# Key sums of three of sixteen blocks by transfers into the other head's sum tile

## The chip, the cores and the metric

The kernel runs on one core of a Trainium2 chip. Its time is the device time of one execution in microseconds; the median of the runs of the kernel before is 2820.77 us (three runs, 2820.2 to 2821.47).

## What is computed

Two blocks are applied to the same input `x` (2048 rows of 1024) and mixed by a gate for each row: A is a linear-attention block, B a softmax-attention block, both with 32 heads of 32 columns.

```python
def _A_ref(x, wqkv, wo):
    qkv = (x @ wqkv).reshape(B, S, 3, H, Dh).transpose(2, 0, 3, 1, 4)
    q, k, v = qkv[0], qkv[1], qkv[2]
    phi = lambda t: jnp.where(t > 0, t + 1, jnp.exp(t)) + 1e-6
    pq, pk = phi(q), phi(k)
    kv = jnp.einsum("bhsd,bhse->bhde", pk, v)
    z = jnp.einsum("bhsd->bhd", pk)
    num = jnp.einsum("bhqd,bhde->bhqe", pq, kv)
    den = jnp.einsum("bhqd,bhd->bhq", pq, z)[..., None] + 1e-6
    return (num / den).transpose(0, 2, 1, 3).reshape(B, S, D) @ wo

def _B_ref(x, wqkv, wo):
    ...
    scores = jnp.einsum("bhqd,bhkd->bhqk", q, k) * (Dh ** -0.5)
    p = _softmax(scores, axis=-1)
    return jnp.einsum("bhqk,bhkd->bhqd", p, v).transpose(0, 2, 1, 3).reshape(B, S, D) @ wo

x = A_x
g = _sigmoid((x * gate_w).sum(-1, keepdims=True))
return g * _A_ref(...) + (1 - g) * _B_ref(...)
```

## The kernel before

PE does all products in fp32 or in three-term products of split operands. After a first part (the projections of B, up to about 620 us) the rest is one long interleaving of four streams, written out in advance by a planner in the kernel's own code: each engine has a booked clock in `T`, `use(engine, cost, ...)` moves it on, and in each turn the main loop takes the stream whose next step can begin soonest by those clocks. So a number such as the cost in `use("pool", 1.23, end)` runs nothing, but decides the order in which instructions stand on every engine.

The streams are:

- **lin** (`linear()`, matmuls L154, L157, L159): the projections of block A, in chunks, first keys and values (kind "kv", beside heads 0 to 14), then queries ("q", heads 14 to 19), then the output of A ("o", heads 19 to 30). At a change of chunk new weights are loaded by SP, split by a ScalarE cast (L1052) and a GpSimd subtraction (L1054) into two parts. For kv chunks the features of the keys are summed over all rows in `zsum` by GpSimd (L1329, L1331).
- **max** (`maxima()`): for each head, 64 score matmuls (L1440), each followed by DVE's row maximum of the bank (L1445). They run one head ahead.
- **head** (`heads_()`): for each head, 16 blocks of 128 keys by four quarters of 512 queries: score matmul (L1581), ScalarE's exp (L1584) into one of nine tiles `pr` of 128x2048, `slot(h, t) = (16 h + t) mod 9`. Blocks 0 to 7 and 8 to 15 are multiplied with the values in two groups (`av`, L1731).
- **out**: the output product of B at the end.

The softmax needs, for each query, the sum of the exps over the keys. It is built from the `pr` tiles in `lacc`, one of two tiles that alternate between heads (`lacc_t[h % 2]`). In heads with `qp = 1536` (all but 15 to 19 and 31), DVE adds the last 512 queries in a PSUM bank (`own`, L1682), and GpSimd the first 1536: block 0 and 1 in `first` (L1662), blocks 2 to 11 in `more` (L1666, 128x1536 each) and blocks 12 to 15 by quarters (`part`, also L1666, 128x512 each), as their exps come by quarters. When all are in, two accumulate DMAs issued by GpSimd fold the tile's halves onto each other (`fold`, L1620 and L1621), and PE sums over the partitions by a product with ones (`finish`, L1504; unfolded, L1496, for heads without fold, among them 30). For head 31 DVE adds everything (L1686).

A `pr` tile may be written again, nine blocks later, once its sums are done and its values multiplied: `pr_left[slot]` holds the marks of the sums still owed, and the head stream waits for them before a block's first score. The sums are queued in `sums_left` and written into GpSimd's order by `add_now` when its clock permits, folds by `fold_now`.

The finish of head h−1 stands on PE ahead of the first `av` group of head h: `av` waits for what is in `ends` and calls it.

## Time and profile before

| | |
|---|---|
| median of the runs | 2820.77 us |
| the profiled execution | 2822.18 us, span 2820.4 us |
| granted clock of PE, mean | 0.998 |
| sum of GpSimd's 128x1536 adds (L1666) | 926.3 us in 264 |
| sum of its 128x512 adds | 487.0 us in 380 |

The profile is that of the profiled execution; engines are PE (matmul), PEld (weight load), DVE, ACT (ScalarE), POOL (GpSimd) and SP. In rows of waits the columns are engine, output and line, what is waited for, then the sum in us, the number of waits and the longest. Rows of windows give the stretch, its length, the busy time of each engine with its instructions, the granted clock of PE, the share of the DMA engines and GB/s. Rows of groups give busy time, mean in ns and the idle time before them. A timeline row begins with start and length in us.

### The profile page before, as it was taken

Reading aid. Unit: us, or ns where it says so; the run is one execution under the profiler, and the core shown is the slowest. Engines: PE = TensorE matmul, PEld = TensorE weight load, DVE = VectorE, ACT = ScalarE, POOL = GpSimd, SP = SyncE. Lnnn points to the kernel's source line nnn. Section 1 sums busy time; section 2 is a strip of 40 time slices with the busy share of each in tenths; the row PEclk is TensorE's granted clock in tenths of the full one; section 3 lists DMA queues with packets and bytes.
Section 4 is the critical chain, followed back from the end, with each engine's and each line's share of the span. In section 5 each row is a group of like instructions: output and inputs, shape, how many; then the busy total and the mean of one; then the engine's idle time right before and its main releaser. Section 6 shows DMA issues by size and latency. Waiting matters only on the chain.

```text
span 2820.4 us, 46781 instructions
## 1 busy us (share of the span) xinstructions
PE 2796.0 (99%) x15784; PEld 2010.3 (71%) x15784; DVE 2268.8 (80%) x3713; ACT 1662.6 (59%) x3170; POOL 2102.9 (75%) x1145
## 2 busy tenths in 40 slices
PE   9999999999999999999999999999999999999999
PEld 8888888886666666676676777667666666666587
DVE  6697759688877888788888778777888888887678
ACT  4343433347666666676776667667767667676522
POOL 0152026459999999999999789989999999999100
PEclk9999999999999999999999999999999999999999
DMA  8588749673433334333344456656544454334674
GB/s 269 166 275 281 225 143 283 218 234 90 123 84 84 92 99 111 93 98 89 88 117 129 152 158 193 183 170 195 136 108 131 107 162 107 92 106 126 233 232 155
DMA packets 391291, 432.77 MB, mean 153 GB/s; under 512 B 105550, under 2 KB 237902, under 8 KB 389260
## 3 DMA queue, kind: packets, MB, share of 16 engines
q1 hardware_dynamic: 367116, 389.27, 45.9%
q0 software_dynamic: 21632, 36.32, 6.1%
q10 hardware_dynamic: 2304, 4.20, 0.4%
q8 instruction: 126, 2.06, 0.3%
q14 instruction: 113, 0.93, 0.1%
HBM read 287.31 MB, written 127.93 MB: 147 GB/s over the span
## 4 chain that ended last, share of the span: by engine, by line
PE 90%; DVE 4%; POOL 3%; DMA 2%; ACT 1%; issue 1%; SPq 0%; DVEq 0%; POOLq 0%; ACTq 0%
PE bank L1731 15%; PE bank L1581 15%; PE bank L1440 15%; PE bank L154 12%; PE bank L157 12%; PE bank L159 12%; PE bank L644 5%; POOL big L1666 3%; DVE mx L1445 2%; DMA big<-ra 1%; PE bank L1504 1%; PE bank L1234 1%; DVE big L1903 1%; DMA big<-big 1%; ACT big L1584 1%
## 5 line engine op out<-in xcount | busy, mean ns | idle before, releaser
L1666 POOL TENSOR_TENSOR big<-big,big 128x512 f32<-128x512 f32 (+2 forms) x694 | 1643.7, 2372 | 61.0 <-ACT big L1584 15.0
L1445 DVE TENSOR_REDUCE mx<-bank 128x1 f32<-128x512 f32 x2048 | 1283.1, 682 | 280.6 <-PE bank L1440 278.3
L1584 ACT ACTIVATE big<-bank 128x512 f32<-128x512 f32 x2048 | 1151.7, 604 | 334.2 <-PE bank L1581 276.1
L1440 PE MATMUL bank<-big,big 128*128 128x512 f32 x1888 | 738.0, 393 | 2.9 <-ACT big L1584 2.2
L1581 PE MATMUL bank<-big,big 128*128 128x512 f32 x1888 | 736.4, 395 | 3.6 <-ACT big L1584 2.9
L154 PE MATMUL bank<-big,big 128*128 128x512 f32 x1408 | 552.8, 393 | 2.6 <-ACT big L304 1.4
L157 PE MATMUL bank<-big,big 128*128 128x512 f32 x1408 | 549.7, 390 | 0.0
L159 PE MATMUL bank<-big,big 128*128 128x512 f32 x1404 | 548.2, 390 | 1.1 <-DVE big L299 1.1
L1731 PE MATMUL bank<-big,mid 128*32 128x512 f32 x4096 | 457.6, 596 | 0.0
L1581 PEld LDWEIGHTS bank<-big,big 128*128 128x128 f32 x1888 | 353.3, 188 | 128.6 <-issue 43.6
L1440 PEld LDWEIGHTS bank<-big,big 128*128 128x128 f32 x1888 | 354.4, 188 | 84.1 <-ACT big L1584 7.7
L1731 PEld LDWEIGHTS bank<-big,mid 128*32 128x32 f32 x4096 | 133.8, 110 | 281.9 <-issue 279.9
L154 PEld LDWEIGHTS bank<-big,big 128*128 128x128 f32 x1408 | 264.8, 188 | 66.8 <-ACT big L1584 5.2
L159 PEld LDWEIGHTS bank<-big,big 128*128 128x128 f32 x1404 | 263.7, 188 | 57.3 <-DVE big L299 2.4
L157 PEld LDWEIGHTS bank<-big,big 128*128 128x128 f32 x1408 | 264.9, 188 | 55.2 <-DVE big L299 0.2
L1682 DVE TENSOR_TENSOR bank<-bank,big 128x512 f32<-128x512 f32 x364 | 252.2, 693 | 13.6 <-ACT big L1584 6.4
L304 ACT CAST big<-mid 128x512 fp32r<-128x512 f32 (+1 forms) x169 | 100.5, 619 | 138.1 <-DVE mid L1850 72.4
L299 DVE TENSOR_TENSOR big<-mid,big 128x512 fp32r<-128x512 f32 (+1 forms) x138 | 96.1, 712 | 78.6 <-ACT big L304 78.1
L644 PE MATMUL bank<-big,big 128*128 128x512 f32 x672 | 152.6, 389 | 0.0
L1662 POOL TENSOR_TENSOR big<-big,big 128x1536 f32<-128x1536 f32 (+1 forms) x31 | 132.9, 4288 | 24.0 <-ACT big L1584 24.0
L644 PEld LDWEIGHTS bank<-big,big 128*128 128x128 f32 x672 | 126.1, 188 | 26.2
L1739 ACT COPY mid<-bank 128x512 f32<-128x512 f32 x32 | 18.8, 588 | 207.9 <-PE bank L1731 180.5
(197 smaller groups left out, 2424.5 us busy)
## 6 DMA issues: line engine op xcount, KB each, us to landing
big<-xs SPq DMA_DIRECT2D x202, 256.0 KB
big<-qk SPq DMA_DIRECT2D x705, 64.0 KB
qk<-mid SPq DMA_DIRECT2D x128, 256.0 KB
xh<-xs SPq DMA_DIRECT2D x102, 256.0 KB
big<-oA SPq DMA_DIRECT2D x86, 256.0 KB
xs<-big SPq DMA_DIRECT2D x64, 256.0 KB
oA<-mid SPq DMA_DIRECT2D x64, 256.0 KB
big<-big POOLq DMA_DIRECT2D x50, 256.0 KB, 5.0
```

Of the source, the lines that this page charges most:

```text
L154: yield nc.tensor.matmul(ps, sh, mh_, start=(kt == 0), stop=False)
L157: yield nc.tensor.matmul(ps, sh, ml_, start=False, stop=(late and last))
L159: yield nc.tensor.matmul(ps, sl, mh_, start=False, stop=last)
L644: nc.tensor.matmul(bank[at + i], x_, w_, start=(kt == u == 0 and not onto), stop=(kt == KH - 1 and u == 2), skip_group_check=onto)
L1440: nc.tensor.matmul(bank[b], q[:, t % TPC * P:(t % TPC + 1) * P], k[:, j * C:(j + 1) * C], start=True, stop=True)
L1445: nc.vector.tensor_reduce(m[:, t, j:j + 1], bank[b], AX.X, ALU.max)
L1581: nc.tensor.matmul(bank[b], k[:, t * P:(t + 1) * P], q_cols(h, j), start=True, stop=True)
L1584: nc.scalar.activation(pr_t[i][:, j * C:(j + 1) * C], bank[b], AF.Exp, scale=SCALE)
L1662: nc.gpsimd.tensor_add(lacc[:, :qp], pr(0)[:, :qp], pr(1)[:, :qp])
L1666: nc.gpsimd.tensor_add(lacc[:, sl], lacc[:, sl], pr(t)[:, sl])
L1682: nc.vector.tensor_add(lacc[:, qp:] if t == NT - 1 else l_b[:, :n], l_b[:, :n], src)
L1731: nc.tensor.matmul(av_b[j * DH:(j + 1) * DH, :], v[:, t, :], pr(t)[:, j * C:(j + 1) * C], start=(t == 0), stop=(t == NT - 1))
```

## The change

In the 25 heads with `qp = 1536` and h < 30 the sums of blocks 8, 9 and 10 (`CHAIN`) are no longer added by GpSimd. Block 8's first 1536 columns are copied by a DMA that ScalarE issues into the other head's sum tile `x`, which is free at that time; blocks 9 and 10 are added to it by accumulate DMAs that GpSimd issues; then one GpSimd add (`total`) puts `x` into `lacc`. Each step is booked behind the landing of the one before (6 us for the copy, 8 us for an accumulate), and each block's `pr` tile is free when its own transfer has landed. The first sum of the next head, which writes `x`, is preceded by what is left of the chain.

Besides, GpSimd's booked costs change (split 1.23 to 1.35, fold 2.0 to 2.45, features 0.69 to 0.78, adds by 0.06, the first add by 0.81), the features' sums are written into GpSimd's order later (`features_now`, at their booked end plus 1.5 us, or when their buffer is due), and in the last head the finish of head 30 no longer stands ahead of the first `av` group but of the second (`early`).

```diff
--- before.py
+++ after.py
@@ -43,6 +43,7 @@
 PIECE_STEPS, PIECE_REST = (4.0, 3.0), 2
 GATE_STEP, GATE_FROM = 2.0, 18.0
 LATE = 1.0
+CHAIN = (8, 9, 10)
@@ -202,6 +203,16 @@
 
     folds = deque()
 
+    chained = deque()
+
+    def chain_now(upto=None):
+
+        while chained and (upto is not None or chained[0][0]() <= T["pe"]):
+            _, fn, mark = chained.popleft()
+            mark.end = fn()
+            if mark is upto:
+                return
+
     def add_later(h, fn):
         mark = Later(None, 0.0, 0.0, 0, None)
         sums_left.append((h, fn, mark))
@@ -222,7 +233,9 @@
     def need(items):
 
         for item in items:
-            if item.end is None and item.fn is None:
+            if item.end is None and any(mark is item for _, _, mark in chained):
+                chain_now(item)
+            elif item.end is None and item.fn is None:
                 add_now(item)
                 assert item.end is not None
             elif item.end is None:
@@ -1050,7 +1063,7 @@
         hi, lo = wpart(k, 0), wpart(k, 1)
         end = use("act", 0.52, at, T["pe"] + LATENCY["pe"])
         nc.scalar.copy(hi, raw)
-        w_ready[k] = use("dve", 0.6, end) if eng is nc.vector else use("pool", 1.23, end)
+        w_ready[k] = use("dve", 0.6, end) if eng is nc.vector else use("pool", 1.35, end)
         eng.tensor_sub(lo, raw, f32(hi))
         raw_free[id(raw)] = w_ready[k]
 
@@ -1207,6 +1220,12 @@
             give(bs[r], 0.0, [defer(low, at)])
 
     z_end = [0.0, 0.0]
+    z_todo = deque()
+
+    def features_now(upto=None):
+        while z_todo and (z_todo[0][0] <= upto if upto is not None else z_todo[0][1] <= T["pe"]):
+            z_todo.popleft()[2]()
+
 
     def keysum(c):
 
@@ -1314,6 +1333,7 @@
                     renew(k)
             extra = iter(())
             e, r = mid[3 + n % 3], mid[6]
+            features_now(n - 3)
             if kind == "kv":
                 va = mid[7][:, (n % 2) * HC:(n % 2 + 1) * HC]
                 yield from keys_alone(n - 2)
@@ -1321,14 +1341,19 @@
                 use("act", 0.28, T["pe"] + LATENCY["pe"])
                 end = phi(ps, e, HC)
 
-                def more(end, c=c, t=t, e=e, ps=ps):
+                def more(end, n=n, c=c, t=t, e=e, ps=ps):
                     pk = e[:, :HC]
                     nc.vector.scalar_tensor_tensor(pk, pk, 1.0, ps[:, :HC], op0=ALU.min, op1=ALU.add)
-                    z_end[c % 2] = use("pool", 0.69, end)
-                    if t == 0:
-                        nc.gpsimd.tensor_copy(zsum[c % 2], pk)
-                    else:
-                        nc.gpsimd.tensor_add(zsum[c % 2], zsum[c % 2], pk)
+                    z_end[c % 2] = None
+
+                    def features():
+                        z_end[c % 2] = use("pool", 0.78, end)
+                        if t == 0:
+                            nc.gpsimd.tensor_copy(zsum[c % 2], pk)
+                        else:
+                            nc.gpsimd.tensor_add(zsum[c % 2], zsum[c % 2], pk)
+
+                    z_todo.append((n, end + 1.5, features))
 
                 todo = [defer(more, end, 0.34)]
                 give(b, 0.0, todo)
@@ -1619,7 +1644,7 @@
             need(lefts)
             nc.gpsimd.dma_start(part(acc, low, 0), part(acc, high, 0), accum_op=ALU.add)
             nc.gpsimd.dma_start(part(acc, high, 1), part(acc, low, 1), accum_op=ALU.add)
-            mark.end = use("pool", 2.0) + 6.0
+            mark.end = use("pool", 2.45) + 6.0
 
         folds.append((h, lambda: ended(lefts), shift))
         return mark
@@ -1629,6 +1654,7 @@
             folds.popleft()[2]()
 
     own_items = []
+    links_of = {-1: []}
 
     def attend(h, lacc):
 
@@ -1649,6 +1675,8 @@
         v = v_tile(h)
         adds, l_left = [], []
         whole = NT - TPC if h + 2 < H else NT
+        links = links_of[h] = []
+        spreads = qp < S and h < H - 2
 
         def idx(t):
             return slot(h, t)
@@ -1656,15 +1684,44 @@
         def pr(t):
             return pr_t[slot(h, t)]
 
+        def spread(t):
+
+            x, n = lacc_t[(h + 1) % 2], CHAIN.index(t)
+            at = pr_end[idx(t)] + LATENCY["act"] + 0.2
+
+            def step():
+                assert finished[0] >= h - 1
+                if n:
+                    nc.gpsimd.dma_start(x[:, :qp], pr(t)[:, :qp], accum_op=ALU.add)
+                    return use("pool", 1.2, T["pe"]) + 8.0
+                nc.scalar.dma_start(x[:, :qp], pr(t)[:, :qp])
+                return use("act", 0.1, T["pe"]) + 6.0
+
+            def total():
+                nc.gpsimd.tensor_add(lacc[:, :qp], lacc[:, :qp], x[:, :qp])
+                return use("pool", 0.21 + qp * 0.0022)
+
+            def after(mark):
+                return (lambda: at) if mark is None else (lambda: max(at, mark.end))
+
+            for fn in (step, total) if t == CHAIN[-1] else (step,):
+                mark = Later(None, 0.0, 0.0, 0, None)
+                chained.append((after(links[-1] if links else None), fn, mark))
+                links.append(mark)
+                l_left.append(mark)
+            pr_left[idx(t)].append(links[n])
+
         def first(at):
 
+            while chained and h > 0 and chained[0][2] in links_of[h - 1]:
+                chain_now(chained[0][2])
             assert finished[0] >= h - 2
             nc.gpsimd.tensor_add(lacc[:, :qp], pr(0)[:, :qp], pr(1)[:, :qp])
-            return use("pool", 0.15 + qp * 0.0022, at)
+            return use("pool", 0.96 + qp * 0.0022, at)
 
         def more(t, at, sl=slice(0, qp)):
             nc.gpsimd.tensor_add(lacc[:, sl], lacc[:, sl], pr(t)[:, sl])
-            return use("pool", 0.15 + (sl.stop - sl.start) * 0.0022, at)
+            return use("pool", 0.21 + (sl.stop - sl.start) * 0.0022, at)
 
         def part(t, j, at):
 
@@ -1693,7 +1750,9 @@
                 else:
                     items = []
             else:
-                if t and t < whole:
+                if spreads and t in CHAIN:
+                    spread(t)
+                elif t and t < whole:
                     at = pr_end[idx(t)]
                     mark = add_later(h, (lambda: first(at)) if t == 1 else (lambda: more(t, at)))
                     l_left.append(mark)
@@ -1714,10 +1773,11 @@
 
         def av(t0, t1):
             blocks_ = range(t0, t1)
+            early = last and t0 == 0
             yield lambda: both(max(pr_end[idx(blocks_[-1])], free[4] if t0 == 0 else 0.0),
-                               *(start() for start, _ in ends))
+                               *(start() for start, _ in ends if not early))
             use("pe", AV_SWITCH, pr_end[idx(blocks_[-1])])
-            while ends:
+            while ends and not early:
                 ends.pop()[1]()
             if bank_at() is not None and bank_at() <= T["pe"]:
                 keys_now(T["pe"])
@@ -2055,6 +2115,8 @@
             advance("head")
         pump_w()
         gate_step()
+        features_now()
+        chain_now()
         fold_now()
         add_now()
         load_w_op()
```

What moves in the order of the instructions is shown at three places. Lines of the new kernel are numbered anew: L1666 is L1723 there, L1662 is L1719, L1054 is L1067, L1331 is L1354, L1440 is L1465, L1581 is L1606, L1496 is L1521, L1731 is L1791, and L154, L157 and L159 are L155, L158 and L160.

GpSimd, the end of head 7 and the beginning of head 8; big_5138 is head 7's sum tile, big_5137 head 8's, and big_221, big_222, big_1258 and big_3332 are the weights to be split. Before:

```order
L1666 TENSOR_TENSOR big_5138<-big_5138,big_5136 128x512
L1666 TENSOR_TENSOR big_5138<-big_5138,big_5128 128x512
L1666 TENSOR_TENSOR big_5138<-big_5138,big_5129 128x512
L1620 DMA big_5138<-big_5138 64x4x256
L1621 DMA big_5138<-big_5138 64x4x256
L1662 TENSOR_TENSOR big_5137<-big_5130,big_5131 128x1536
L1054 TENSOR_TENSOR big_221<-big_5140,big_221 128x512
L1331 TENSOR_TENSOR mid_230<-mid_230,mid_227 128x256
L1054 TENSOR_TENSOR big_221<-big_5140,big_221 128x512
L1054 TENSOR_TENSOR big_222<-big_5140,big_222 128x512
L1054 TENSOR_TENSOR big_222<-mid_224,big_222 128x512
L1054 TENSOR_TENSOR big_1258<-mid_225,big_1258 128x512
```

The same place now:

```order
L1695 DMA big_5137<-big_5133 128x1536
L1723 TENSOR_TENSOR big_5138<-big_5138,big_5136 128x512
L1723 TENSOR_TENSOR big_5138<-big_5138,big_5128 128x512
L1723 TENSOR_TENSOR big_5138<-big_5138,big_5129 128x512
L1723 TENSOR_TENSOR big_5138<-big_5138,big_5135 128x512
L1067 TENSOR_TENSOR big_221<-big_5140,big_221 128x512 x2
L1067 TENSOR_TENSOR big_222<-big_5140,big_222 128x512
L1701 TENSOR_TENSOR big_5138<-big_5138,big_5137 128x1536
L1354 TENSOR_TENSOR mid_230<-mid_230,mid_227 128x256
L1067 TENSOR_TENSOR big_222<-mid_224,big_222 128x512
L1067 TENSOR_TENSOR big_1258<-mid_225,big_1258 128x512
L1067 TENSOR_TENSOR big_1258<-big_5140,big_1258 128x512
```

The splits stood behind the fold (L1620, L1621) and head 8's first add; they now stand among head 7's last adds, the second accumulate (L1695) and the total (L1701), and the fold follows six rows later.

PE, the last head's first `av` group; big_5137 is head 30's sum tile, bank_242 the output of `av`. Before:

```order
L154 MATMUL bank_240<-big_1258,big_210 128x512
L157 MATMUL bank_240<-big_1258,big_210 128x512
L1496 MATMUL bank_243<-big_5137,ones 32x512 x4
L1731 MATMUL bank_242<-big_5129,mid_236 32x512 x4
L1731 MATMUL bank_242<-big_5130,mid_236 32x512 x4
L1731 MATMUL bank_242<-big_5131,mid_236 32x512 x4
L1731 MATMUL bank_242<-big_5132,mid_236 32x512 x4
```

The same place now:

```order
L155 MATMUL bank_243<-big_1258,big_210 128x512
L158 MATMUL bank_243<-big_1258,big_210 128x512
L1791 MATMUL bank_242<-big_5129,mid_236 32x512 x4
L1791 MATMUL bank_242<-big_5130,mid_236 32x512 x4
L1791 MATMUL bank_242<-big_5131,mid_236 32x512 x4
L1791 MATMUL bank_242<-big_5132,mid_236 32x512 x4
L1606 MATMUL bank_244<-big_208,big_209 128x512
```

And 28 rows further down PE, where L1496 (now L1521) stands:

```order
L160 MATMUL bank_239<-big_221,big_210 128x512
L155 MATMUL bank_239<-big_222,big_210 128x512
L158 MATMUL bank_239<-big_222,big_210 128x512
L1521 MATMUL bank_241<-big_5137,ones 32x512 x4
L1791 MATMUL bank_242<-big_5133,mid_236 32x512 x4
```

The finish moved from ahead of the first group to ahead of the second, with 31 single matmuls and the first group between.

PE, head 28, from its twelfth score on, that is where block 3 begins; output banks rotate. Before:

```order
L1581 MATMUL bank_240<-big_206,big_207 128x512
L1440 MATMUL bank_244<-big_209,big_208 128x512
L1581 MATMUL bank_239<-big_208,big_207 128x512
L1440 MATMUL bank_242<-big_209,big_208 128x512
L159 MATMUL bank_243<-big_3332,xh 128x512
L1581 MATMUL bank_241<-big_206,big_207 128x512
L1440 MATMUL bank_240<-big_209,big_208 128x512
L154 MATMUL bank_238<-big_221,big_210 128x512
L1581 MATMUL bank_239<-big_206,big_207 128x512
L157 MATMUL bank_238<-big_221,big_210 128x512
L1440 MATMUL bank_244<-big_209,big_208 128x512
L1581 MATMUL bank_243<-big_206,big_207 128x512
```

Now:

```order
L1606 MATMUL bank_241<-big_206,big_207 128x512
L1465 MATMUL bank_239<-big_209,big_208 128x512
L1465 MATMUL bank_243<-big_209,big_208 128x512
L1465 MATMUL bank_242<-big_209,big_208 128x512
L160 MATMUL bank_240<-big_3332,xh 128x512
L1465 MATMUL bank_244<-big_209,big_208 128x512
L1465 MATMUL bank_241<-big_209,big_208 128x512
L155 MATMUL bank_238<-big_221,big_210 128x512
L158 MATMUL bank_238<-big_221,big_210 128x512
L160 MATMUL bank_238<-big_221,big_210 128x512
L1465 MATMUL bank_239<-big_209,big_208 128x512
L1465 MATMUL bank_240<-big_209,big_208 128x512
```

Where scores and maxima took turns, five scores and four maxima, one score and seven maxima stand in twelve rows now, three of these in a row and then two and two; the scores follow behind in twos and fours. Such places stand right behind the twelfth score of heads 2, 5, 8, 12, 23, 25, 28 and 30, and others in heads 2, 5, 8, 9, 20, 21 and 25.

## The prediction

> **What bounds the kernel now.** I read the page's busy line first, then the waits of PE, then the groups of POOL, then the stretches of the span in which PE does not run freely.
>
> ```profile
> PE 2796.0 (99%) x15784; PEld 2010.3 (71%) x15784; DVE 2268.8 (80%) x3713; ACT 1662.6 (59%) x3170; POOL 2102.9 (75%) x1145
> PE bank L1496 <- POOL big L1666: 5.4, 1, 5.4
> PE bank L1581 <- ACT big L1584: 2.9, 1, 2.9
> PE bank L1440 <- ACT big L1584: 2.2, 2, 1.4
> PE bank L1504 <- DMA big<-big: 1.8, 2, 1.1
> PE bank L1504 <- POOL big L1054: 0.8, 1, 0.8
> 2440.00:2450.00 10.00, 10.00 (x45) 1.00 0.78 164
> 2512.00:2570.00 58.00, 58.00 (x340) 39.10 (x336) 49.49 (x84) 39.44 (x72) 56.13 (x26) 1.00 0.37 93
> ```
>
> PE is the bound: 2796.0 of 2820.4 us. The change gives PE no matmul more and none less, so the time can move only by what PE stalls. A free stretch (2440 to 2450) holds 45 matmuls in 10 us, 0.222 us each; I price every disturbed stretch against that. The last row is an ordinary head of the o stage, with PE, PEld, DVE, ACT and POOL in that order: PE has no idle time, and POOL is busy 56.13 of 58 us. So POOL, not PE's bound, is full from head to head, and where it has extra work (weight splits, features, the end) somebody waits for it. That is the list of waits above: four of the five longest lead to POOL or to the fold's transfers that POOL issues.
>
> **What the change takes from POOL.** The groups of POOL, by form:
>
> ```profile
> L1666 POOL TENSOR_TENSOR big<-big,big 128x1536 f32<-128x1536 f32 x264 | 926.3, 3509 | 18.5
> L1666 POOL TENSOR_TENSOR big<-big,big 128x512 f32<-128x512 f32 x380 | 487.0, 1289 | 24.1
> L1621 POOL DMA_DIRECT2D big<-big x25 | 34.2, 1369 | 1.3 <-PE bank L1581 0.7 <-issue 0.6
> L1620 POOL DMA_DIRECT2D big<-big x25 | 25.2, 1010 | 7.2 <-POOL big L1666 7.2
> 2559.27 1.01 POOL L1620 DMA_DIRECT2D big<-big  x1 [0.30 <-POOL big L1666]
> 2559.92 1.40 POOL L1621 DMA_DIRECT2D big<-big  x1
> 2560.55 4.30 POOL L1662 TENSOR_TENSOR big<-big,big 128x1536 f32<-128x1536 f32 x1
> ```
>
> In each of 25 heads three adds of 128x1536 go and one comes back (the total): 2 x 3.51 = 7.02 us less. Two accumulate DMAs come. Their busy time by the fold's rows is 1.01 to 1.37 us, but the timeline shows the next instruction starting 0.64 us after each (2559.27, 2559.92, 2560.55). So POOL gains 4.3 to 5.7 us per head; I take 5. That lowers 56 to about 51 of 58 us. In the kv and o heads POOL then has slack to swallow a run of weight splits or features, which it now hands on as a wait.
>
> **What goes.** First the end. Head 30's finish (L1496) waits for POOL's last add, and PE then restarts at a lower clock:
>
> ```profile
> 2615.56 1.94 PE bank L1496 x8
> 2617.49 3.92 PE bank L1731 x32
> 2628.76 3.57 PE bank L1731 x32
> 2615.00:2619.00 4.00, 3.44 (x20) 0.58 0.98 383
> ```
>
> The wait is 5.44 us, and in the 3.44 us after it the granted clock is 0.58, which loses 3.44 x 0.42 = 1.4 us. The order shows L1496 moved behind the first AV group and 31 single matmuls: 3.57 + 31 x 0.222 = 10.5 us later, twice the wait. So 6.8 us go even if POOL were no faster. What is late next is the next AV group, which now stands behind L1496; POOL's sums of head 30 have 5 us of new margin there too.
>
> Second, head 8, where the weight splits stand behind adds, fold and first add in POOL's queue. SP waits for them, the raw weights come late, and ScalarE's casts hold up its exps:
>
> ```profile
> SPq L171 <- POOL big L1054: 12.2, 1, 12.2
> 1138.50:1149.00 10.50, 6.21 (x19) 0.84 0.58 170
> 1141.44 0.62 ACT L1052 CAST big<-big 128x512 fp32r<-128x512 f32 x1 [3.54 <-DMA big<-in_a_wqkv]
> 1143.57 4.43 POOL L1054 TENSOR_TENSOR big<-big,big 128x512 fp32r<-128x512 f32 x3
> ```
>
> 10.5 - 19 x 0.222 = 6.3 us are lost. After the change these splits stand in head 7's row of POOL, before the fold, so I let all 6.3 go.
>
> Third, the folded finishes that wait for a fold issued late:
>
> ```profile
> 772.40 0.59 PE L1504 MATMUL bank<-big,ones 64*32 64x256 f32 x2 [0.78 <-POOL big L1054]
> 774.11 0.66 PE L1504 MATMUL bank<-big,ones 64*32 64x256 f32 x14 [1.12 <-DMA big<-big]
> 771.30:776.50 5.20, 3.30 (x46) 0.87 0.43 108
> ```
>
> The waits of L1504 sum to 1.8 + 0.8 = 2.6 us; the clock of 0.87 over 5.2 us costs another 0.7, and the group's broken start about as much again: 4.0. Together 6.8 + 6.3 + 4.0 = **17.1 us** go.
>
> **What comes.** A freed pr slot now hangs on the landing of a transfer. Slot of block 10 is that of block 3 in the next head, and its accumulate is the last of three in a row. Where head scores must wait, PE runs maxima (L1440) instead, several in a row, and later scores in a row. A maximum needs DVE, whose reduction is slower than PE. Before has stretches of just this kind:
>
> ```profile
> L1445 DVE TENSOR_REDUCE mx<-bank 128x1 f32<-128x512 f32 x2048 | 1283.1, 682 | 280.6 <-PE bank L1440 278.3
> 795.00:801.00 6.00, 5.16 (x20) 1.00 0.13 36
> 864.04:868.87 4.83, 4.46 (x15) 1.00 0.55 157
> 925.93:933.92 7.99, 7.80 (x31) 1.00 0.25 75
> ```
>
> A reduction takes 682 ns against 222 of a matmul, so a run of maxima is DVE's pace. The three stretches lose 6.00 - 20 x 0.222 = 1.6, 4.83 - 15 x 0.222 = 1.5 and 7.99 - 31 x 0.222 = 1.1 us. I count, over PE's whole order, each L1440 that follows another directly: 39 before, 102 after. The 39 cost 4.2 us, 0.11 each; the 13 in the last two stretches cost 2.6, 0.20 each. For 102 that is 11.2 to 20.4 us. I take 0.13, nearer to the mean of all, since most of the new ones stand in twos and threes, as most of the old did: 13.3. Since the old 4.2 are within it, **9.1 us** come.
>
> **The transfers.** No row shows 768 KB within SBUF. The nearest are the folds, a third of the size, and SP's issues:
>
> ```profile
> big<-big POOLq DMA_DIRECT2D x50, 256.0 KB, 5.0
> 1149.67 0.32 SPq L171 DMA_DIRECT2D big<-qk  x1
> L1331 POOL TENSOR_TENSOR mid<-mid,mid 128x256 f32<-128x256 f32 x45 | 36.8, 818 | 11.4 <-DVE mid L1326 7.0 <-issue 3.9 <-ACT big L1584 0.4
> ```
>
> The bounds of a landing are 5.0 us (size costs nothing) and 15.0 (three times). I take about 7.5, nearer to 5.0, since the fold moves runs of 256 values and the chain runs of 1536, and a part of the 5.0 doesn't grow with size. At that, the booked 8 us hold, and what the planner shows as a free slot is free.
> The Trainium skill speaks to this in "DMA: Bandwidth & Descriptors", section "Anatomy of one DMA — SWDGE (gpsimd) path": a fixed 2.0 us and then bytes at 436 GB/s. For 786,432 bytes that is an estimate of 3.8 us by that page, and the bookings would hold with much to spare. For the fold's 262,144 bytes the same rule gives 2.6 us, and the trace has 5.0, so the trace does not agree, and the measurement decides.
>
> ScalarE's 25 plain copies cost an issue each, 0.32 us by SP's row, 8 us in all beside an engine that is busy 59%; behind the copy stand the next exps. It waits for the finish that last read the tile, which PE has passed some scores earlier, so I put it at nothing; were the finish late, PE would be standing there anyway. The later features are short POOL operations (0.82 us a piece) whose results are needed at the end of a chunk; POOL's slack hides them. Changed bookings cost nothing by themselves: they move orders, which the counts above hold. DMA engines are at 0.37 in the head shown; three transfers of 7.5 us in 58 us, were each to fill all engines, add at most 0.39.
>
> **The sum.** The profiled execution took 2822.18 us with a span of 2820.4; the runs' median is 2820.77, 1.4 below it. Span: 2820.4 - 17.1 + 9.1 = 2812.4; profiled run 2814.2; median **2813 us**.
>
> **The rivals.**
> 1. *The runs of maxima eat the gain.* At 0.20 each they come to 20.4, and if half of head 8's loss stays (3.2) the sum is 2820.77 - 13.9 + 16.2 = 2823; with 0.17 and all of head 8 gone it is 2817. For it: eleven heads of the new order (2, 5, 8, 9, 12, 20, 21, 23, 25, 28, 30) have four or more such followers, before three (2, 3, 4), head 0 apart, which is alike. Against: outside the three stretches the old ones cost nothing that I can find. Here 2815 to 2823.
> 2. *The accumulates land later than booked* (the slower side). Eight heads (2, 5, 8, 12, 23, 25, 28, 30) have a patch of maxima right behind their twelfth score, where block 3's are due, so there the order left no room. Each microsecond over 8 is paid there once per head, since ScalarE's first exp of block 3 stands in front of all other exps, and PE has few banks. The gain of 8 is used up at 8 + 8/8 = 9 us. At 10 us it costs 8 x 2 = 16, 2829; at 11 it is 2837. At 15, other heads pay as well. For it: three times the size, and an engine share that rises to 0.78 in places. Against: long runs per row.
> 3. *POOL isn't relieved*: it stands at the second accumulate until the first has landed and at the total until the second has. Then head 8 and the folds stay, the end's 6.8 goes by the order alone, and the time is 2820.77 - 6.8 + 9.1 = 2823, no change. Six 512-wide adds (6 x 1.29 = 7.7 us) stand between the links in the order, which speaks against it if a landing is under 8.
> 4. *The runs cost what their long ones cost.* After has six runs of four or more, 25 followers at 0.20: 5 us. Then 2820.77 - 17.1 + 5.0 - 4.2 = 2804.
>
> **How the numbers follow.** My forecast (2808 to 2815) has a chance of 0.42, rival 4 (2803 to 2808) 0.14, rival 1 0.22, rival 3 0.08, rival 2 0.14. A measurement of this kernel can tell about 0.2% from no change, 5.6 us: faster is below 2815.1, slower above 2826.4. Faster: 0.42 + 0.14 = 0.56, and a little of rival 1, 0.57. Slower: rival 2 from 9.7 us on (8 x 1.7 = 13.6), 0.13. Same: 0.30. The range leaves out the tail of rival 2 and what lies below 2803: 2803 to 2828. The likeliest case's own range is 2808 to 2815.
>
> **What would show it.** L1496 has no wait in the list, and the clock stays at 1.00 around it. SP's wait for L1054 in head 7 or 8 is under 5 us. POOL's busy time falls by 100 to 140 us. big<-big lands in 7 to 8 us and ScalarE issues 25 of them. Waits of L1581 or L1440 for ScalarE right before block 3 in those eight heads mean rival 2; the same places at DVE's pace, with waits for L1445, mean rival 1. POOL idle for DMA above 2 us a head at the links means rival 3. I would be wrong altogether if PE lost time at places that neither order shows as a run or a wait.

## The result, and the profile after

The changed kernel takes **2852.18 us** (median of four runs, 2847.96 to 2852.86), before 2820.78: a ratio of 1.0108, with a 95% interval of 1.0091 to 1.0126. It is 31 us slower. The forecast was 2813, with a range to 2828: the sign was wrong.

The page of the changed kernel: the busy line, the transfers of GpSimd's queue, and the two rows of the chain's transfers (times issued, KB each, us from issue to landing).

```profile
PE 2814.4 (99%) x15784; PEld 2004.2 (70%) x15784; DVE 2263.8 (79%) x3713; ACT 1653.6 (58%) x3170; POOL 1970.2 (69%) x1145
...
q0 software_dynamic: 28832, 75.64, 13.4%
...
big<-big POOLq DMA_DIRECT2D x50, 768.0 KB, 6.9
...
big<-big ACTq DMA_DIRECT2D x25, 768.0 KB
```

GpSimd was relieved as forecast (2102.9 to 1970.2, 132.7 us less), and a link (one of the chain's transfers) lands in 6.9 us by the median, near the forecast's 7.5. The waits of PE show something that the prediction did not have:

```profile
PE bank L1606 <- DMA extra<-ml: 6.5, 3, 5.4
PE bank L1606 <- DMA big<-big: 5.8, 1, 5.8
PE bank L1606 <- DMA big<-ml: 4.6, 2, 4.0
PE bank L1465 <- ACT big L1609: 3.2, 5, 1.7
PE bank L1529 <- DMA big<-big: 1.4, 1, 1.4
```

L1606 is the score matmul, L1609 its exp (L1584 before), L1465 the maxima's matmul, L1529 the folded finish (L1504 before). Three times the first score of a head (8, 21, 24) waits 4 to 6 us, for `ml`: the two row vectors `mh` and `ml` with the maxima, 2 and 6 KB each, which SP copies into the head's query tiles (in the second row, for head 24, the row names another transfer of that time; the semaphores, read below, show that it was `ml` there too). The wait for GpSimd at head 30's finish is gone.

To see where the time went I summed, for each head, the stalls of PE: for every matmul the distance to the next one's start, less the usual distance of its kind. A wait ahead of a head's first score counts to the head before. Heads in which nothing moves are left out.

| stalls of PE, us, by head | 2 to 4 | 5 | 7, 8 | 9, 10 | 20, 21 | 22 to 25 | 31 | all heads |
|---|---|---|---|---|---|---|---|---|
| before | 15.0 | 0.5 | 8.9 | 1.2 | 3.1 | 3.2 | 13.7 | 64.3 |
| after | 11.9 | 4.5 | 19.3 | 3.1 | 12.8 | 17.1 | 6.6 | 95.5 |

31.2 us more in all, which is the whole difference: 10 in heads 7 and 8, 10 in 20 and 21, 14 in 22 to 25, 4 in 5, 2 in 9 and 10; and 7 less at the end, 3 less in heads 2 to 4.

How a head comes to wait for its rows is seen in the timeline of PE and SP of the changed kernel, at the end of head 23 (start, length, engine, line; L1482 is PE's transpose of the maxima, L1606 head 24's first score):

```profile
2201.45 1.76 SPq L172 DMA_DIRECT2D wa<-mid  x2
2203.31 1.15 SPq L172 DMA_DIRECT2D ra<-mid  x1
2204.51 2.99 SPq L172 DMA_DIRECT2D wa<-mid  x2
...
2209.16 0.27 PE L1482 MATMUL bank<-ident,mneg 128*16 128x128 f32 x1
...
2214.08 0.64 SPq L172 DMA_DIRECT2D big<-mh  x1
2214.81 0.64 SPq L172 DMA_DIRECT2D big<-ml  x1
2215.50 1.39 SPq L172 DMA_DIRECT2D big<-mh  x1
2216.94 1.34 SPq L172 DMA_DIRECT2D big<-ml  x1
...
2221.90 0.76 PE L1606 MATMUL bank<-big,big 128*128 128x512 f32 x1 [5.82 <-DMA big<-big]
```

The five SP issues shown first take 5.9 us, beside the second link (issued at 2201.47, landed at 2208.41). SP's queue is behind, and the rows are first issued 4.9 us after the transpose. The first pair, 2 KB each, fills the tile of the first 512 queries, which the first score reads; the second pair, 6 KB each, is for the later scores. By the semaphores that the score waits for, it is the 2 KB of `ml`, issued at 2214.81, that lands last, at 2221.77, 7.0 us later, and PE goes on at 2221.90. Behind the wait PE runs slower for a while: the granted clock is 0.60 in the next 6.1 us.

### The profile page after: what moved, and what is told of

Same layout as the page of the kernel before. It is cut to its first block, busy times and chain, and to the rows that moved or that the text cites. A ratio compares the mean times of both kernels' runs of the same rounds, so it can differ in the third digit from the quotient of the medians.

```text
span 2851.1 us, 46804 instructions
## 1 busy us (share of the span) xinstructions
PE 2814.4 (99%) x15784; PEld 2004.2 (70%) x15784; DVE 2263.8 (79%) x3713; ACT 1653.6 (58%) x3170; POOL 1970.2 (69%) x1145
## 4 chain that ended last, share of the span: by engine, by line
PE 88%; DVE 6%; DMA 2%; issue 1%; POOL 1%; ACT 1%; SPq 0%; POOLq 0%; ACTq 0%; DVEq 0%
PE bank L1791 16%; PE bank L1606 15%; PE bank L1465 13%; PE bank L155 12%; PE bank L158 12%; PE bank L160 12%; PE bank L657 5%; DVE mx L1470 5%; ACT big L1609 1%; DVE bank L1739 1%; PE bank L1529 1%; PE bank L1253 1%; POOL big L1723 1%; POOL big L1067 1%; DMA big<-ra 0%
## 5 line engine op out<-in xcount | busy, mean ns | idle before, releaser
L1723 POOL TENSOR_TENSOR big<-big,big 128x512 f32<-128x512 f32 (+2 forms) x619 | 1388.3, 2247 | 120.3 <-ACT big L1609 82.8
L1609 ACT ACTIVATE big<-bank 128x512 f32<-128x512 f32 x2048 | 1143.0, 605 | 378.1 <-PE bank L1606 324.7
L1606 PE MATMUL bank<-big,big 128*128 128x512 f32 x1888 | 733.8, 397 | 12.0 <-DMA big<-big 5.8
L1465 PE MATMUL bank<-big,big 128*128 128x512 f32 x1888 | 735.9, 396 | 6.4 <-ACT big L1609 3.2
L155 PE MATMUL bank<-big,big 128*128 128x512 f32 x1408 | 552.4, 392 | 2.3 <-ACT big L317 1.4
L158 PE MATMUL bank<-big,big 128*128 128x512 f32 x1408 | 549.7, 390 | 0.0
L160 PE MATMUL bank<-big,big 128*128 128x512 f32 x1404 | 548.4, 391 | 0.8 <-DVE big L312 0.8
L1791 PE MATMUL bank<-big,mid 128*32 128x512 f32 x4096 | 458.8, 597 | 0.0
L1606 PEld LDWEIGHTS bank<-big,big 128*128 128x128 f32 x1888 | 353.1, 188 | 140.8 <-issue 55.1
L1465 PEld LDWEIGHTS bank<-big,big 128*128 128x128 f32 x1888 | 354.4, 188 | 100.8 <-DVE mx L1470 18.0
L1791 PEld LDWEIGHTS bank<-big,mid 128*32 128x32 f32 x4096 | 130.9, 111 | 286.6 <-issue 284.6
L155 PEld LDWEIGHTS bank<-big,big 128*128 128x128 f32 x1408 | 264.5, 188 | 66.7 <-ACT big L1609 4.4
L160 PEld LDWEIGHTS bank<-big,big 128*128 128x128 f32 x1404 | 263.9, 188 | 56.3 <-DVE big L312 2.1
L158 PEld LDWEIGHTS bank<-big,big 128*128 128x128 f32 x1408 | 264.5, 188 | 55.0 <-DVE big L312 0.4
L1719 POOL TENSOR_TENSOR big<-big,big 128x1536 f32<-128x1536 f32 (+1 forms) x31 | 130.3, 4204 | 33.2 <-ACT big L1609 32.3
```

The source lines that it names most:

```text
L155: yield nc.tensor.matmul(ps, sh, mh_, start=(kt == 0), stop=False)
L158: yield nc.tensor.matmul(ps, sh, ml_, start=False, stop=(late and last))
L160: yield nc.tensor.matmul(ps, sl, mh_, start=False, stop=last)
L1465: nc.tensor.matmul(bank[b], q[:, t % TPC * P:(t % TPC + 1) * P], k[:, j * C:(j + 1) * C], start=True, stop=True)
L1606: nc.tensor.matmul(bank[b], k[:, t * P:(t + 1) * P], q_cols(h, j), start=True, stop=True)
L1609: nc.scalar.activation(pr_t[i][:, j * C:(j + 1) * C], bank[b], AF.Exp, scale=SCALE)
```

## The experiments

Two theories were set against each other. **T**: the links' size; while they run, SP's small transfers are issued and land late, the rows above all. **O**: the order of the instructions that the new planning makes, with its runs of maxima, whatever the transfers cost. Later runs ask which link it is and which parts of the change are worth anything. A follower is a maximum (L1465) that stands directly behind another on PE; each run's order has its count. Kernels of one group ran beside runs of the kernel before; its median was 2820.6 to 2821.7.

**No chain**

```diff
-CHAIN = (8, 9, 10)
+CHAIN = ()
```

> The changed kernel with an empty list of chained blocks: blocks 8 to 10 are added by GpSimd as before; the new bookings, the later features and the moved finish of head 30 stay. Theory T (the transfers): the first scores of heads 8, 21 and 24 waited 5.4, 4.0 and 5.8 us for the small row transfers (mh, ml), which landed 5 to 6 us after their issue instead of 1.5 to 3, because the 768 KB transfers fill the DMA engines; without the chain these waits are gone and the end's 7 us stay won: about 2812 to 2818. Theory O (the order): the bookings and the later features by themselves make runs of maxima and late rows: 2830 or more.

2854.1 us, 1.0115 (1.0098 to 1.0131): the 2812 to 2818 of T is missed, the 2830 or more of O holds. No wait for rows is left, but others are:

```profile
PE bank L1529 <- DMA big<-big: 9.9, 7, 3.2
PE bank L1606 <- ACT big L1609: 8.2, 2, 7.4
```

With GpSimd at its full load the new durations and the rest of the change lose as much as the chain does in another way: 19.8 us of stalls in heads 7 and 8, 14.7 in 9 and 10.

**The same order with small links** (the output lacks most of the sums of three blocks)

```diff
-nc.gpsimd.dma_start(x[:, :qp], pr(t)[:, :qp], accum_op=ALU.add)
+nc.gpsimd.dma_start(x[:, :HC], pr(t)[:, :HC], accum_op=ALU.add)
...
-nc.scalar.dma_start(x[:, :qp], pr(t)[:, :qp])
+w = HC if h else qp
+nc.scalar.dma_start(x[:, :w], pr(t)[:, :w])
```

> The changed kernel in the same order on every engine, but each link of the chain moves 256 columns instead of 1536 (the copy of head 0 apart), so most of the sums of blocks 8 to 10 are left out. Theory T: the row transfers land within 3 us again, the waits for mh and ml (16 us in the list) are gone, with the slow restart behind them some 20 us: about 2830. Theory O: the order is unchanged, so the time is too: 2848 to 2853. What is left above 2821 minus 7 for the end is then the order's own cost.

2832.5 us (1.0024 to 1.0054): 19.7 us of the loss are the size of the transfers. The other 11.7 are the order's, with what the small transfers still cost. The split is not clean: of the waits below, 4.8 us are head 7's finish waiting for its fold, and in the changed kernel that wait is 1.4.

```profile
PE bank L1529 <- DMA big<-big: 5.2, 3, 3.2
```

The same place as above, the end of head 23, in this kernel:

```profile
2192.11 0.96 SPq L172 DMA_DIRECT2D wa<-mid  x2
2193.18 0.38 SPq L172 DMA_DIRECT2D ra<-mid  x1
2193.60 1.01 SPq L172 DMA_DIRECT2D wa<-mid  x2
...
2199.77 0.27 PE L1482 MATMUL bank<-ident,mneg 128*16 128x128 f32 x1
...
2201.41 0.64 SPq L172 DMA_DIRECT2D big<-mh  x1
2202.15 0.58 SPq L172 DMA_DIRECT2D big<-ml  x1
2202.78 0.77 SPq L172 DMA_DIRECT2D big<-mh  x1
2203.59 0.73 SPq L172 DMA_DIRECT2D big<-ml  x1
```

The five issues take 2.35 us, not 5.9, the first row is issued 1.6 us after the transpose, and head 24 begins without a wait. Over heads 20 to 29 SP's issues take 0.463 us in the mean here, 0.544 in the changed kernel, 0.456 before.

**The rows by another engine**

```diff
-dma(f32(q[r:r + 1, :]).rearrange(...), f32(part[ts]))
+T["sp"] = max(T["sp"], T["pe"]) + DMA_ISSUE
+nc.scalar.dma_start(f32(q[r:r + 1, :]).rearrange(...), f32(part[ts]))
```

> The changed kernel with the row transfers (mh, ml) issued by ScalarE instead of SP, order otherwise the same. If the rows wait behind other transfers of SP's own queue, which the chain only slows: they land within 3 us and the waits are gone, about 2832. If every queue suffers because the engines themselves are busy: they land as late as before, 2848 to 2855. Rival: ScalarE stands at the transfers for DVE's ml, and exps behind it are late: 2855 or more.

2977.2 us (1.0538 to 1.0572). The rival held, and hides the question: ScalarE, whose next exp (L1610 here) stands behind them, waits at these transfers, and PE for its exps (L1607 is the score here).

```profile
ACT big L1610 <- DMA big<-mh: 48.1, 13, 6.1
PE bank L1607 <- ACT big L1610: 56.3, 18, 5.9
PE bank L1465 <- ACT big L1610: 37.8, 15, 5.0
```

Whether a queue of their own would help the rows is left open.

**The moved finish alone**

```diff
+early = last and t0 == 0
...
-while ends:
+while ends and not early:
```

> The kernel before with nothing changed but the finish of head 30 moved behind the last head's first group. Both theories: the wait of 5.4 us for GpSimd and the slow restart go, 6.8 us: about 2814. If the next group waits for it instead: 2819 to 2821.

2822.6 us (0.9995 to 1.0014): nothing. PE's wait for GpSimd is gone and another has come, since the finish's last step (L1517, which frees its bank) stands behind DVE's adds for the last head:

```profile
PE bank L1581 <- DVE mid L1517: 3.8, 1, 3.8
```

DVE's timeline at that place, with the 26 adds ahead of L1517:

```profile
2610.33 19.02 DVE L1686 TENSOR_TENSOR big<-big,big 128x512 f32<-128x512 f32 x26
2629.28 0.67 DVE L1517 TENSOR_TENSOR mid<-mid,bank 128x512 f32<-128x512 f32 x1
```

**The new durations alone**, the two that weigh most shown:

```diff
-use("pool", 0.15 + qp * 0.0022, at)
+use("pool", 0.96 + qp * 0.0022, at)
...
-w_ready[k] = ... use("pool", 1.23, end)
+w_ready[k] = ... use("pool", 1.35, end)
```

> The kernel before with only GpSimd's new booked durations (split, fold, first, more, features). Every engine does the same work; 121 maxima follow a maximum directly, 39 before. Theory O (the durations alone remake the order, and an order planned with GpSimd overbooked costs what the kernel without the chain showed): 2845 to 2862, with stalls at heads 2, 8, 9, 10 and 20. Rival F (the later features did it there): 2819 to 2828.

2877.3 us (1.0185 to 1.0215), slower than expected. Durations that run nothing cost 57 us when nothing relieves GpSimd: 24.7 us of stalls in heads 7 and 8, 28.8 in 2 to 4.

**Two links**

```diff
-CHAIN = (8, 9, 10)
+CHAIN = (8, 9)
```

> The changed kernel with blocks 8 and 9 chained and block 10 added by GpSimd: one accumulate a head instead of two, ended some 8 us earlier in the head, well ahead of the row transfers of the next. 45 maxima follow a maximum. Theory T (the third transfer lies on the row transfers): the waits for mh and ml are under 3 us in all, and with few runs 2811 to 2820. Rival: any large transfer hits the rows, or GpSimd is as full as without the chain: 2832 or more.

2815.0 us, 0.9980 (0.9970 to 0.9989): faster than before. The waits for `ml` are 4.0 us, where T had under 3. One link more, and the order that the planner makes with it (102 followers for 45), turn the change from 6 us of gain to 31 of loss; what each of the two does is not separated here.

**Three links with the old durations**: the diff's five numbers set back.

> The changed kernel with GpSimd's old booked durations; chain, later features and moved finish stay. 122 followers, 102 in the change. Theory T: the rows are hit by the third transfer here as well, waits for mh and ml of 10 us and more, 2842 to 2858. Rival B (the new durations are what made the changed kernel slow): 2815 to 2830.

2867.2 us (1.0144 to 1.0178). The new durations are not what made the change slow; with three links they save 15 us. 12.4 us of waits for `ml` remain, as theory T had it, though the time is beyond its range.

**The rows booked later**

```diff
-rows_ready[h] = end + 2.5
+rows_ready[h] = end + 6.5
```

> The changed kernel with the row transfers booked to land 6.5 us after DVE's row maximum instead of 2.5, as they do beside the third transfer; nothing else. Theory T: the planner puts other work there, the waits for mh and ml fall from 16 to under 4 us, but 143 maxima follow a maximum instead of 102: 2838 to 2848. Rival: the rows' lateness is not to be covered, since nothing else can run: 2850 or more.

2852.7 us (1.0101 to 1.0131), no gain. The waits for `ml` fell from 11.1 us (16.9 with the one of head 24) to 4.9; by the balance the 41 additional followers took it back. That the order can't absorb this lateness is what the rival said.

**Which link?** First the third small and the others whole, then the reverse, in the order of the change (in each, sums of the small links are left out in part).

```diff
-nc.gpsimd.dma_start(x[:, :qp], pr(t)[:, :qp], accum_op=ALU.add)
+w = qp if n == 1 else HC
+nc.gpsimd.dma_start(x[:, :w], pr(t)[:, :w], accum_op=ALU.add)
```

> The changed kernel in the same order, but the third link (block 10) moves 256 columns instead of 1536, so most of that block's sums are left out; copy and second link are whole. Theory T3 (it is the third transfer, since it lies on the row transfers at the head's end): nearly all of the 19.7 us of the run with small links come back, 2831 to 2837. Rival G (each transfer costs its share, wherever it lies): a third of it, 2843 to 2847.

2842.2 us (1.0058 to 1.0088): 10.0 of the 19.7 us are gone, between the two expectations.

```diff
+w = qp if n == 2 else HC
...
+w = HC if h else qp
```

> The changed kernel in the same order with the copy and the second link small (256 columns, head 0's copy apart) and the third whole: the counterpart of the run with the third small, which took 10.0 of the 19.7 us away. Theory A (the transfers' cost adds up, each delays what SP moves beside it): 2842, the third alone brings 10 back. Rival Q (the delay comes of transfers that queue behind each other, so the third alone finds the engines free): 2833 to 2837.

2832.1 us (1.0023 to 1.0052), the time with all links small. So the cost doesn't add up: the third alone costs nothing that can be told from noise, copy and second link alone 9.7 us, all three 19.7. The traces show how, at the three heads whose first score waited. The first figure is the time in us from PE's transpose to the issue of the 2 KB of `ml`, the second that from there to its landing, by the semaphore's updates in the trace; in brackets PE's wait.

| | head 8 | head 21 | head 24 |
|---|---|---|---|
| before | 4.4 + 2.6 (0) | 3.2 + 1.6 (0) | 3.2 + 2.1 (0) |
| all links small | 4.4 + 2.5 (0) | 3.5 + 1.6 (0) | 2.4 + 2.4 (0) |
| third alone whole | 4.4 + 2.1 (0) | 3.7 + 1.6 (0) | 2.8 + 2.5 (0) |
| copy and second whole | 6.7 + 2.3 (2.1) | 8.0 + 1.6 (0.7) | 4.9 + 2.5 (0.5) |
| all whole, the change | 7.0 + 5.4 (5.4) | 7.9 + 5.0 (4.0) | 5.7 + 7.0 (5.8) |

Copy and second link make the issue late, by 2.3 to 4.5 us against small links, and leave the landing as it was. The late row is then issued behind the third link (0.6, 1.4 and 1.3 us behind it in the changed kernel), and lands 3.1 to 4.4 us later beside a whole third link than beside a small one. With the third alone whole the row is issued 1.5 to 1.9 us ahead of it and lands in time. These are three heads in one trace of each kernel.

**Blocks 9 and 10**

```diff
-CHAIN = (8, 9, 10)
+CHAIN = (9, 10)
```

> The changed kernel with blocks 9 and 10 chained and block 8 added by GpSimd: as many transfers as in the run with blocks 8 and 9 (2815), 46 followers instead of 45, but the accumulate lies one block (3.6 us) later, nearer to the row transfers. Theory T3: the waits for mh and ml rise from 4 to 8 us or more, 2819 to 2828. Rival: place doesn't matter, 2812 to 2817.

2818.7 us (0.9979 to 0.9999). The waits for `ml` are 6.0 us, 4.0 with blocks 8 and 9. Nearer to the rows is worse, but the two intervals overlap; inconclusive by time.

**Weight splits behind the adds**

```diff
+while eng is nc.gpsimd and chained:
+    chain_now(chained[0][2])
+while eng is nc.gpsimd and sums_left:
+    add_now(sums_left[0][-1])
```

> The changed kernel, but what is left of the chain and of GpSimd's adds is written ahead of a weight split. Up to head 7 the order is that of the change. Theory S (in the change the splits stand ahead of the total, GpSimd idles 17 us there, and head 8's finish is late): GpSimd's idle time moves behind the fold, the stalls of head 8 fall from 12.9 to 6 or less; the whole is 2844 to 2850, as later heads get 24 more followers. Rival: head 8 loses as much, since the splits are late in either place: 2852 or more.

2863.3 us (1.0147 to 1.0163), slower than expected in all, since the order after head 8 changed for the worse (12.1 us of stalls in head 14). In head 8 itself the stalls fell from 12.9 to 7.5, with 16 followers in both. GpSimd's timeline at the end of head 7, in the changed kernel (L1067 is the split, L1701 the total, L1645 the fold):

```profile
1111.84 5.43 POOL L1723 TENSOR_TENSOR big<-big,big 128x512 f32<-128x512 f32 x4
1134.25 3.80 POOL L1067 TENSOR_TENSOR big<-big,big 128x512 fp32r<-128x512 f32 x3 [16.98 <-ACT big L1065]
1137.99 3.52 POOL L1701 TENSOR_TENSOR big<-big,big 128x1536 f32<-128x1536 f32 x1
1153.26 1.03 POOL L1645 DMA_DIRECT2D big<-big  x1 [0.30 <-POOL big L1723]
```

GpSimd stands 17 us at the first split, for a cast of ScalarE (L1065), with the total, three adds and the fold behind it. With the splits behind (here the total is L1705, the fold L1649, the split L1071):

```profile
1117.38 3.47 POOL L1705 TENSOR_TENSOR big<-big,big 128x1536 f32<-128x1536 f32 x1 [0.88 <-DMA big<-big]
1125.25 1.03 POOL L1649 DMA_DIRECT2D big<-big  x1 [0.30 <-POOL big L1727]
1130.03 3.29 POOL L1071 TENSOR_TENSOR big<-big,big 128x512 fp32r<-128x512 f32 x2
```

the fold goes 28 us earlier. Head 8 then loses about what it lost before the change (8.0), not less.

**Two links with the old durations**

> Blocks 8 and 9 chained, with GpSimd's old booked durations: 17 maxima follow a maximum, 45 with the new ones. Theory O (a follower costs some 0.26 us, as the run with small links had it): 7 us below 2815, about 2808, if waits for mh and ml stay as they are. Rival B (bookings shorter than the trace put work behind GpSimd too early): waits for GpSimd or for a fold come instead, 2815 to 2822.

2809.4 us, 0.9955 (0.9940 to 0.9970), with 17 followers. What it lost to the links' size was tried in its order, again with 256 columns:

> Two links with the old bookings in the same order, each link 256 columns: most of the sums of blocks 8 and 9 are left out. The waits for mh and ml, 5.8 us there, and the slow restart behind head 8's should go: 2799 to 2803 against 2809.4. If the row transfers were late for another reason (SP's own queue): 2807 to 2810.

2797.8 us (0.9900 to 0.9930), further than expected: 11.6 us. No wait for `ml` is left, where there were two rows:

```profile
PE bank L1606 <- DMA big<-ml: 3.2, 3, 1.3
PE bank L1606 <- DMA extra<-ml: 2.6, 1, 2.6
```

**Parts of the change beside two links**: the finish where it was, and the features' sums at once.

```diff
-early = last and t0 == 0
+early = False
```

> Two links with the old bookings, but the finish of head 30 ahead of the last head's first group, as before the change. If the moved finish is worth what the prediction said: 2815 to 2817. If the relieved GpSimd ends head 30's sums in time by itself: 2808 to 2811.

```diff
-z_todo.append((n, end + 1.5, features))
+features()
```

> Two links with the old bookings, but the features' sums written into GpSimd's order at once, as before the change. 20 followers against 17. If the later features matter: 2813 or more, with GpSimd waiting for DVE at L1354 and PE behind it. If not: 2808 to 2811.

2810.7 us (0.9948 to 0.9977) and 2808.5 us (0.9941 to 0.9971): both parts are worth nothing that can be told here.

**Links only where GpSimd was waited for**, two links and old durations in both:

```diff
-spreads = qp < S and h < H - 2
+spreads = qp < S and (h < 14 or H - 5 <= h < H - 2)
```

> Two links with the old bookings, but only in heads 0 to 13 and 27 to 29: in heads 20 to 26 nobody waited for GpSimd before the change, while with links these heads lost 6 to 7 us more than before. Theory T: those come back and the end stays won, 2802 to 2806 against 2809.4. Rival: GpSimd enters the last heads late again and the end's wait returns: 2809 or more.

2804.0 us, 0.9938 (0.9921 to 0.9954).

```diff
+spreads = qp < S and (h < 4 or 7 < h < 10 or H - 5 <= h < H - 2)
```

> As the run before, with links only in heads 0 to 3, 8, 9 and 27 to 29. Theory T: head 8's wait for the rows (2.6 us) goes too, 2799 to 2805, if GpSimd isn't late for head 8's weight splits. Rival: without links in heads 4 to 7 the splits meet a full GpSimd as before the change, head 8 loses 6 to 8 us again: 2807 or more.

**2800.2 us**, 0.9927 (0.9912 to 0.9942), faster than both kernels by 20 and 52 us. Nine heads with links instead of 25, 2080.1 us of GpSimd instead of 1970.2, and no wait for rows in the list.

| stalls of PE, us, by head | 2 to 4 | 5 | 7, 8 | 9, 10 | 20, 21 | 22 to 25 | 31 | all heads |
|---|---|---|---|---|---|---|---|---|
| small links, order of the change | 11.8 | 4.4 | 16.9 | 3.1 | 7.4 | 6.7 | 6.5 | 75.3 |
| two links | 9.4 | 0.5 | 7.6 | 2.1 | 8.4 | 5.9 | 6.5 | 58.0 |
| two links, old durations | 7.0 | 0.7 | 7.8 | 1.4 | 4.1 | 6.4 | 6.9 | 53.3 |
| the same, small | 6.4 | 0.6 | 3.3 | 1.8 | 2.0 | 3.3 | 6.7 | 41.6 |
| two links in nine heads | 6.9 | 0.6 | 4.1 | 1.5 | 2.2 | 3.9 | 6.6 | 43.3 |

## Why the prediction was wrong

- *That PE is the bound and only its stalls can move* held: the difference in stalls, 31.2 us, is the difference in time.
- *That GpSimd is relieved by 5 us a head* held: 132.7 us in 25 heads, 5.3 each. Rival 3, which had it not relieved, fell.
- *The end* held in size (13.7 to 6.6 us), not in its reason. "So 6.8 us go even if POOL were no faster" is wrong: the moved finish alone gave nothing, and beside two links its absence costs nothing. What it takes is that GpSimd ends sooner or that the order around it changes, as it did in the run without chain.
- *Head 8, 6.3 us* failed, and the step is "I let all 6.3 go". I read from the order that the splits now stand before the fold, and took the earlier place for an earlier time. An earlier place in the queue of an engine that must wait for its input is a place in which it blocks: GpSimd stood 17 us there (9.9 with small links), the fold behind it was late, and PE waited for it. Instead of 6.3 less the order gave head 8 some 8 us more (8.0 to 16.0 with small links). With the splits behind the fold again it was 7.5, so the place of the splits cost it; the 6.3 did not go in that run either.
- *The folded finishes, 4.0 us*, came out about so: 3.1 in heads 2 to 4.
- *The runs of maxima* were mis-sized: 0.13 us a follower. With small links, heads 5, 9, 12, 20, 21, 23, 25, 28 and 30, which have 55 followers, lost 14.5 us more than before, 0.26 each. This is a mean over heads that differ much, from under 0.1 in heads 12 and 21 to some 0.4 in 5 and 20, and head 8's 16 followers are not in it. The new ones came in patches, like the two stretches with 0.20; that this makes them dearer is likely, but was not measured.
- *The transfers* failed, and this is the largest part. Their landing was right, 6.9 us against some 7.5, so rival 2 was not what happened: the maxima's waits for ScalarE are 3.2 us, and 3.3 with small links that land in 3.1. What they do to others was left out. The prediction added up shares of the DMA engines ("at most 0.39") and found room; it never asked which small transfer PE waits for at that time. The rows were the one: before they landed in time for the head, now they don't. The transfers' size costs 19.7 us, shown by the same order with small links. The listed waits for rows, with that of head 24, are 16.9 us; the slower clock behind them is part of the rest, which was not split further. The prediction's own sign of being "wrong altogether", time lost where neither order shows a run or a wait, is what came.

With the measured sizes the prediction's own sum closes, as it must nearly, since they are parts of the same stalls: 7.1 and 3.1 less, 8 and 14.5 more for the order makes 12.3, where the run with small links shows 11.7, and 19.7 for the size of the transfers makes 32, where 31.4 was measured.

The Trainium skill has the rule that was wanted: "DMA: Bandwidth & Descriptors", section "Issuing engines are not separate DMA queues", says that transfers of ScalarE, SP and GpSimd run on the same 16 DMA engines and interleave whoever issued them. The traces agree: SP's `ml` lands in 5.0 to 7.0 us beside a whole link of GpSimd's queue, in 1.6 to 2.5 beside or ahead of a small one. The formula of the same page, section "Anatomy of one DMA — SWDGE (gpsimd) path", that the prediction weighed gives 3.8 us for a link by an estimate, and the landing is 6.9; the measurement decides.

## What to carry to other kernels

Before a large transfer is put where an engine has room, look for the small transfer that the busiest engine waits for at that time, and price the large one by it, not by its own landing or by a share of bandwidth. Here it was a small transfer issued behind the large one that landed late; one issued ahead of it did not. An instruction that comes earlier in the queue of an in-order engine is only earlier if its input is. Relief belongs where somebody waits: with two links and the old durations nine heads gave 20 us and 25 heads 12, while 25 with three links lost 31.

## What was not expected of the hardware

Issuing itself slows under load: SP's five issues at the end of head 23 took 5.9 us beside a whole link and 2.35 in the same place of the order with small ones. And the links' cost does not add up: the third alone costs nothing that can be told, the first two 9.7 us, all three 19.7.
